# A bias tile of 512 bytes in place of 32, in an attention kernel with two expert layers

## The chip, the cores and the metric

The kernel runs on one core of a Trainium2 chip. The metric is the device time of one execution in microseconds (us), as the median of the runs shown. Engines are called as in the profile: PE is TensorE's matmul, PEld its weight load, DVE is VectorE, ACT is ScalarE, POOL is GpSimd, SP issues most of the DMAs. About 0.3% (3.1 us here) is what a measurement of this kernel can tell from no change.

## The reference

Attention with a compressive memory over 4 batches, 8 heads, 576 positions and 64 columns a head; its result, as 2304 tokens by 512 columns, goes through two expert layers.

```python
def _attn_ref(q, k, v, M_prev, z_prev, beta):
    scores = scale * q @ k.T                    # causal, softmax -> a
    local = a @ v
    q_p = phi(q)                                # elu + 1
    mem_out = (q_p @ M_prev) / (q_p @ z_prev + 1e-6)
    g = sigmoid(beta)
    return g * mem_out + (1 - g) * local

def _moe_ref(x, w_in, w_out):                   # 2304x512, 512x2048, 2048x512
    h = x @ w_in
    return (h * np.cos(h)) @ w_out

def _moe2_ref(x, w_in, w_out):                  # the same shapes
    h = x @ w_in
    r = np.maximum(h, 0.0)
    return (r * r) @ w_out
```

## The kernel before, in words

The first 206 us are attention: 16 units (a batch and a pair of heads), one after the other, each with its scores, exponentials, transposes and products. Its result goes to DRAM and comes back as the tiles of x. Beside attention run the first conversions of weights, which arrive as 64-bit floats.

Then come the expert layers. The tokens are cut into five blocks: 512, 512, 512, 256, 512 (blocks 0 to 4). The 2048 inner columns are cut into 16 groups f = 0 to 15. One step s is one block and one f: function l1 (matmuls at line 267, output h) makes 128 inner columns from x, functions g_a to g_g (lines 280 to 328) turn h into the expert function's value, split in a high part gh and a low part gl, and l2 (matmuls at line 762, output a) adds its product with w_out into accumulators. l2 runs two steps behind l1. The order of steps is block 0 with f 0 to 7, block 1 with all f, block 0 with f 8 to 15, then blocks 2, 3, 4; that is the first layer. The second layer takes blocks 0, 1, 2, 4, 3.

All matmuls of the expert layers work on pairs of high and low parts: high by high, high by low and low by high. For l1 a step has 4 x 3 = 12 matmuls. The stationary operand is a slice of 128 columns (512 bytes in a partition) of winh or winl of group f, the moving operand is xh or xl with 512 columns (256 in block 3). For l2 the first layer has 12 matmuls a step: stationary a slice of wouth or woutl, moving gh or gl. In the second layer the roles change: stationary is a slice of gh or gl, moving is wouth or woutl with 512 columns, and a step has 12 matmuls (6 in block 3, whose 256 tokens make two slices). PE runs the 12 of l1 of one step and the 12 of l2 of another in turns, at times with one dozen cut in two by the other.

Tiles lie in SBUF in the order in which their pools are made: wA (line 114: weights of f = 0 to 3), wr (115: raw and half-made weights), xs (116: x tiles, xh, xl), cst (117: halfpi alone, line 124), gp and g3 (276, 277: gf, ki, gh, gl), and then the pools of attention (336 to 338), which end with attention and make room for go (903: output tiles) and wB (904: weights of f = 4 to 15). Every tile of wA, wr, gp, g3, go and wB has a multiple of 512 bytes in a partition; the two of 2304 bytes in xs make 4608 together, and lie ahead of xh and xl. Only halfpi is smaller: 4 bytes, for which 32 are set aside.

```python
    cst = ctx.enter_context(tc.tile_pool(name="cst", bufs=1))
    NA = CFG["NA"]                          # 4
    wpool = [wA] * NF
    halfpi = cst.tile([128, 1], F32, name="halfpi")
...
    wB = ctx.enter_context(tc.tile_pool(name="wB", bufs=1))
    for f in range(NA, NF):
        wpool[f] = wB
```

So before the change wA, wr, xh and xl have one address mod 512, and gf, ki, gh, gl, the output tiles and the weights of f = 4 to 15 another, 32 bytes on.

The tile halfpi is written once by POOL (line 647) and read as the bias of the cosine (line 308).

Of the kernel before, what the change touches and what calls it, by code (L numbers as in the profile page):

```python
# [9 lines left out]
F32 = mybir.dt.float32  # L10
# [75 lines left out]
def kernel(  # L86
# [30 lines left out]
    cst = ctx.enter_context(tc.tile_pool(name="cst", bufs=1))  # L117
# [3 lines left out]
    NA = CFG["NA"]  # L121
    NSP = NF
    wpool = [wA] * NF
    halfpi = cst.tile([128, 1], F32, name="halfpi")
    wt = {}

    pe, act, dve, pool = nc.tensor, nc.scalar, nc.vector, nc.gpsimd
# [207 lines left out]
    def attention(ctx):  # L335
# [7 lines left out]
        pe, act, dve, pool = (_Pinned(tc, e) for e in (nc.tensor, nc.scalar, nc.vector, nc.gpsimd))  # L343
# [300 lines left out]
            )  # L644
        for t in (t[:, S:] for t in (*qpb, *Pl)):
            pool.memset(t, 0.0)
        pool.memset(halfpi, math.pi / 2)
        nc.scalar.dma_start(out=ig, in_=beta.rearrange("(o h) -> o h", o=1).partition_broadcast(128))

        def gates():  # L650
# [87 lines left out]
        pe, act, dve, pool = nc.tensor, nc.scalar, nc.vector, nc.gpsimd  # L738
# [162 lines left out]
    with ExitStack() as actx:  # L901
        attention(actx)
# [58 lines left out]
```

## Time and profile before

| | us |
|---|---|
| median of 3 runs | 1023.69 |
| lowest and highest run | 1021.48, 1024.98 |
| span of the profiled execution, first to last instruction | 1022.1 |
| PE busy in it | 997.3 |
| mean granted clock of PE | 0.995 |

The span is one execution; the runs are others. A busy share of PE counts a matmul up to a modelled end, so the time that a matmul takes of PE is read from the starts: a row of the chain of waits that holds 12 matmuls in a run lasts from the start of its first to the start of what comes next. The letters "PE h L267" stand for l1's matmuls and "PE a L762" for l2's. The granted clock is 1.00 at 2.4 GHz and 0.5 at 1.2 GHz.

### The profile page before, as it was taken

The numbers are of one execution on the slowest core, as the hardware profiler recorded it, in microseconds if no ns is written. First come the engines' busy times: TensorE is split into PE (matmuls) and PEld (weight loads), VectorE is DVE, ScalarE is ACT, GpSimd is POOL, SyncE is SP. The second block draws the span as 40 slices with busy tenths as digits, with TensorE's granted clock in tenths as the row PEclk, the third lists the DMA queues.
The fourth block names the chain that finished last, engine by engine and source line by source line (L and its number), as shares of the span: only waits on it lengthen the run. The fifth ranks groups of instructions, "written<-read, shape, count | busy, mean of one in ns | idle before, by whom it ended". The sixth has DMA issues, their size and how long they took to land.

```text
span 1022.1 us, 14853 instructions
## 1 busy us (share of the span) xinstructions
PE 997.3 (98%) x5456; PEld 800.8 (78%) x5456; DVE 597.1 (58%) x1217; ACT 545.3 (53%) x1120; POOL 240.1 (23%) x294
## 2 busy tenths in 40 slices
PE   8999999889999899999999999999999999999998
PEld 5777777667777688888997777888888888888897
DVE  6888898668998766446564799624222322322232
ACT  6988987677777565436565776413212322321232
POOL 5776865274331100000005544200000000000000
PEclk9999999999999999999999999999999999999999
DMA  6456655352435642002023235002000100100010
GB/s 203 142 155 187 208 195 162 116 184 83 144 119 191 201 139 73 1 1 83 1 63 113 83 102 196 21 1 62 21 1 20 53 1 1 52 1 1 1 42 21
DMA packets 53736, 88.00 MB, mean 86 GB/s; under 512 B 9504, under 2 KB 29344, under 8 KB 53664
## 3 DMA queue, kind: packets, MB, share of 16 engines
q1 hardware_dynamic: 53088, 86.57, 26.6%
q8 instruction: 43, 0.70, 0.3%
q10 hardware_dynamic: 576, 0.50, 0.1%
q14 instruction: 29, 0.24, 0.1%
HBM read 66.07 MB, written 20.97 MB: 85 GB/s over the span
## 4 chain that ended last, share of the span: by engine, by line
PE 74%; DVE 10%; ACT 6%; DMA 5%; issue 3%; POOL 2%; SPq 0%; DVEq 0%; ACTq 0%; POOLq 0%
PE h L267 29%; PE a L762 28%; PE o L47 5%; PE sps L47 5%; PE ptps L47 4%; PE qps L47 1%; DVE wb L169 1%; DVE gf L300 1%; DVE wa L173 1%; DMA xraw<-xT 1%; DMA wf<-ws2in 1%; DVE gl L325 1%; DVE wa L165 1%; DVE gf L292 1%; DMA wraw<-in_moe_w_in_dram 1%
## 5 line engine op out<-in xcount | busy, mean ns | idle before, releaser
L267 PE MATMUL h<-xh,winh 128*128 128x512 f32 (+1 forms) x628 | 234.5, 374 | 5.6 <-DVE gf L313 3.5
L267 PE MATMUL h<-xl,winh 128*128 128x512 f32 (+1 forms) x628 | 234.1, 373 | 0.0
L267 PE MATMUL h<-xh,winl 128*128 128x512 f32 (+1 forms) x628 | 233.7, 372 | 0.0
L325 DVE TENSOR_TENSOR gl<-gf,gh 128x512 fp32r<-128x512 f32 (+1 forms) x158 | 107.8, 683 | 124.1 <-ACT gh L318 123.9
L318 ACT ACTIVATE gh<-gf 128x512 fp32r<-128x512 f32 (+1 forms) x158 | 92.1, 584 | 113.4 <-PE a L762 95.8
L267 PEld LDWEIGHTS h<-xh,winh 128*128 128x128 f32 x628 | 118.2, 189 | 31.0 <-DVE gf L313 5.6
L267 PEld LDWEIGHTS h<-xh,winl 128*128 128x128 f32 x628 | 118.6, 189 | 22.6
L267 PEld LDWEIGHTS h<-xl,winh 128*128 128x128 f32 x628 | 118.5, 189 | 22.4
L296 DVE TENSOR_TENSOR gf<-gf 128x512 f32<-128x512 f32 (+1 forms) x80 | 53.5, 672 | 137.5 <-ACT gf L288 137.4
L288 ACT ACTIVATE gf<-h 128x512 f32<-128x512 f32 (+1 forms) x80 | 43.8, 552 | 153.0 <-PE h L267 152.4
L762 PE MATMUL a<-gl,wouth 128*128 128x512 f32 (+1 forms) x320 | 116.9, 372 | 3.0 <-DVE gl L325 3.0
L762 PE MATMUL a<-gh,woutl 128*128 128x512 f32 (+1 forms) x320 | 116.3, 369 | 0.0
L762 PE MATMUL a<-woutl,gh 128*128 128x512 f32 x288 | 112.9, 392 | 0.0
L762 PE MATMUL a<-wouth,gl 128*128 128x512 f32 x288 | 112.9, 392 | 0.0
L762 PE MATMUL a<-wouth,gh 128*128 128x512 f32 x288 | 98.7, 392 | 0.0
L762 PE MATMUL a<-gh,wouth 128*128 128x512 f32 (+1 forms) x320 | 86.3, 374 | 4.3 <-ACT gh L318 2.4
L47 POOL TENSOR_SCALAR P<-P,sm 128x512 f32<-128x512 f32 (+3 forms) x128 | 78.9, 634 | 38.4 <-DVE sm L47 22.2
L313 DVE TENSOR_TENSOR gf<-h,gf 128x512 f32<-128x512 f32 (+1 forms) x78 | 49.3, 633 | 52.5 <-PE h L267 37.9
L286 ACT ACTIVATE ki<-h 128x512 int32<-128x512 f32 (+1 forms) x77 | 42.1, 547 | 57.0 <-DVE gf L313 50.3
L762 PEld LDWEIGHTS a<-gl,wouth 128*128 128x128 f32 x320 | 60.2, 188 | 15.7 <-DVE gl L325 5.3
L762 PEld LDWEIGHTS a<-gh,wouth 128*128 128x128 f32 x320 | 56.4, 188 | 18.5 <-ACT gh L318 4.8
L47 ACT ACTIVATE P<-P,mx 128x384 f32<-128x384 f32 (+3 forms) x127 | 69.5, 551 | 0.0
(111 smaller groups left out, 1558.0 us busy)
## 6 DMA issues: line engine op xcount, KB each, us to landing
wraw<-in_moe_w_in_dram SPq DMA_DIRECT2D x32, 512.0 KB, 3.9
wraw<-in_moe_w_out_dram SPq DMA_DIRECT2D x32, 512.0 KB, 3.5
qk<-in_qk_dram SPq DMA_DIRECT2D x15, 640.0 KB, 5.4
vr<-in_vrow_dram SPq DMA_DIRECT2D x16, 320.0 KB, 4.4
xT<-x SPq DMA_DIRECT2D x16, 288.0 KB, 4.4
out_dram<-ob SPq DMA_DIRECT2D x17, 256.0 KB, 2.3
x1T<-ob SPq DMA_DIRECT2D x16, 256.0 KB, 2.9
xraw<-x1T SPq DMA_DIRECT2D x16, 256.0 KB, 2.7
```

The lines of the kernel that those rows point to most:

```text
L47: made = call(*args, **kwargs)
L165: lambda: dve.tensor_scalar(out=a, in0=a, scalar1=3, scalar2=0x3FFFFFF8, op0=ALU.logical_shift_left, op1=ALU.bitwise_and,),
L169: lambda: dve.scalar_tensor_tensor(out=b, in0=hi, scalar=-0x40000000, in1=a, op0=ALU.bitwise_and, op1=ALU.bitwise_or),
L173: lambda: dve.tensor_tensor(out=a, in0=b, in1=r, op=ALU.add),
L267: pe.matmul(out=h[:, 0:n], lhsT=lt[:, kk * 128:(kk + 1) * 128], rhs=rt[:, 0:n], start=(kk == 0 and x == 0), stop=(kk == KD - 1 and x == 2),)
L286: act.activation(out=kis[s], in_=hs[s], func=AF.Copy, scale=1.0 / TWO_PI)
L288: act.activation(out=rs[s], in_=hs[s], func=AF.Relu)
L296: dve.tensor_tensor(out=rs[s], in0=rs[s], in1=rs[s], op=ALU.mult)
L313: dve.tensor_tensor(out=rs[s], in0=hs[s], in1=rs[s], op=ALU.mult)
L318: act.activation(out=gh, in_=rs[s], func=AF.Copy)
L325: eng.tensor_tensor(out=gl, in0=rs[s], in1=gs[s].bitcast(F32), op=ALU.subtract)
L762: nc.tensor.matmul(out=o, lhsT=lt, rhs=rt, start=((p, j, f) in opens and x == 0), stop=((p, j, f) in closes and x == 2),)
```

## The change

The tile halfpi gets 128 columns in place of one, 512 bytes in place of 32, and the write of its value names its first column. All tiles that lie behind it start 480 bytes later.

```diff
@@ -121,7 +121,7 @@
     NA = CFG["NA"]
     NSP = NF
     wpool = [wA] * NF
-    halfpi = cst.tile([128, 1], F32, name="halfpi")
+    halfpi = cst.tile([128, 128], F32, name="halfpi")
     wt = {}
 
     pe, act, dve, pool = nc.tensor, nc.scalar, nc.vector, nc.gpsimd
@@ -644,7 +644,7 @@
             )
         for t in (t[:, S:] for t in (*qpb, *Pl)):
             pool.memset(t, 0.0)
-        pool.memset(halfpi, math.pi / 2)
+        pool.memset(halfpi[:, 0:1], math.pi / 2)
         nc.scalar.dma_start(out=ig, in_=beta.rearrange("(o h) -> o h", o=1).partition_broadcast(128))
```

## Rows read from the trace of the kernel before

**Rows 1.** Page, part 1: busy time, share of the span, instructions.
```profile
PE 997.3 (98%) x5456; PEld 800.8 (78%) x5456; DVE 597.1 (58%) x1217; ACT 545.3 (53%) x1120; POOL 240.1 (23%) x294
```

**Rows 2.** Busy time by stretches, PE alone: stretch, length, busy (matmuls), clock, DMA, GB/s.
```profile
206.00:356.00 150.00, 141.23 (x591) 0.99 0.47 151
342.90:346.40 3.50, 3.50 (x10) 0.51 0.13 20
346.40:494.00 147.60, 146.90 (x698) 1.00 0.21 70
...
556.00:621.00 65.00, 62.18 (x265) 1.00 0.34 105
621.00:1022.00 401.00, 397.21 (x1812) 1.00 0.08 28
```

**Rows 3.** Waits of PE, 206 to 356 us: total us, times, longest us.
```profile
PE h L267 <- DVE gf L313: 2.3, 2, 2.1
PE a L762 <- DVE gl L325: 2.1, 4, 1.1
```

**Rows 4.** Waits of PE, 540 us to the end.
```profile
PE h L267 <- DVE gf L313: 1.2, 1, 1.2
PE a L762 <- DVE gl L325: 1.0, 1, 1.0
```

**Rows 5.** Chain of waits, second layer: start us, us, what.
```profile
885.35 1.62 PE a L762 x7
886.97 2.75 PE h L267 x12
...
895.27 2.80 PE a L762 x12
898.07 2.73 PE h L267 x12
...
904.06 2.80 PE a L762 x12
909.20 2.80 PE h L267 x12
...
915.26 2.72 PE a L762 x12
...
926.34 2.72 PE a L762 x12
```

**Rows 6.** Chain of waits, first layer, block 2: two runs of 24.
```profile
422.87 5.60 PE h L267 x24
428.47 5.47 PE a L762 x24
```

**Rows 7.** Instructions on tile halfpi: count, then duration ns, minimum, median, maximum.
```profile
L47 POOL MEMSET halfpi<- x1: 92/92/92, 3.7 to 3.7; 128x1 f32 x1
```

**Rows 8.** Chain of waits, block 3 (256 columns) in both layers.
```profile
476.85 2.88 PE h L267 x24
...
496.33 2.84 PE h L267 x24
...
973.33 1.42 PE h L267 x12
```

**Rows 9.** Waits of DVE, 206 to 540 us.
```profile
DVE gf L313 <- PE h L267: 32.2, 17, 6.9
```

**Rows 10.** Groups of DVE, up to 206 us and from 206 to 610 us.
```profile
L47 DVE SCALAR_TENSOR_TENSOR wb<-wraw,wa 128x512 int32<-128x512 int32 x16 | 11.2, 698 | 0.0
...
L169 DVE SCALAR_TENSOR_TENSOR wb<-wraw,wa 128x512 int32<-128x512 int32 x38 | 29.6, 779 | 0.4
```

**Rows 11.** Attention: stretch, length, busy of PE, PEld, DVE, ACT, POOL, clock.
```profile
0.00:206.00 206.00, 198.01 (x1748) 144.89 (x1748) 167.53 (x548) 168.28 (x444) 123.45 (x192) 0.98 0.54 171
```

**Rows 12.** Timeline of PE after its longest wait: start us, us, instruction.
```profile
343.38 0.63 PE L267 MATMUL h<-xl,winh 128*128 128x512 f32 x1
343.81 0.63 PE L267 MATMUL h<-xh,winl 128*128 128x512 f32 x1
```

## The prediction, made before the changed kernel was run

> **What bounds the kernel now.** I read the page's busy times first: PE is busy 98% of the span [rows 1], far ahead of the others. A share says little of where PE is late, so next come the stretches. From 621 us on PE is busy to the end but for the tail of outputs (397.2 of 401 us), and from 346 to 494 us for 146.9 of 147.6; there every nanosecond of a matmul is a nanosecond of the kernel [rows 2]. From 206 to 356 us and from 556 to 621 us PE stands idle for 8.8 and 2.8 us, because DVE and ACT come late with gf, gl and gh [rows 2, 3, 4]; a faster PE may only wait longer there. Third, the chain of waits shows how long a dozen matmuls takes from start to start. That is the view that decides this case, because the kernel before already holds both kinds of addresses.
>
> Which kind a row is follows from the order of steps. In [rows 5], from the second layer's block 4, the h rows are f = 1, 3, 5 and the dozens of a are f = 0 and 1, 2, 4, 6 (the piece of 7 ahead of them is f = 15 of the block before). x and the weights of f < 4 have equal addresses mod 512, so h of f = 1, 3 is an equal pair and h of f = 5 an unequal one. For a it is the other way round: gh and gl lie 32 bytes on, equal to the weights of f >= 4, unequal to those of f < 4. The rows follow this both ways: h takes 2.75 and 2.73 us where equal and 2.80 where not, a takes 2.80 where unequal and 2.72 where equal [rows 5]. Of the 62 runs of exactly 12 between 621 and 966 us, 32 read 2.79 or 2.80 (the unequal ones) and 30 read 2.72 to 2.75 (the equal ones). The first layer, in which gh moves and the weight stands, shows the same: 24 of h with f = 7, 8 take 5.60 us, 24 of a with f = 5, 6 take 5.47 [rows 6]. The clock is 1.00 in all of them [rows 2].
>
> **The change, part by part.** The removed and added operations cost nothing: POOL's write stays one column, of 0.09 us at 3.7 us into the span, long before the first cosine [rows 7]. No instruction, wait or DMA is added or moved in the program's text. What changes is where tiles lie: gf, ki, gh, gl, the output tiles and the weights of f >= 4 move by 480 bytes, and then all operands of l1 and l2 are equal mod 512.
>
> *Matmuls that become equal pairs.* By the loops, a block of 512 tokens has 12 steps of 12 h (f >= 4) and 4 steps of 12 a (f < 4) that are unequal: 192 of 384. The first layer has four such blocks, 768; the second four and the 4 x 6 a of its block of 256, 792. An unequal one takes 2.80 / 12 = 233.3 ns. What an equal one will take is bounded by 2.75 and 2.72 us a dozen: 229.2 and 226.7 ns [rows 5]. Equal dozens that unequal ones cut in two are slower: a piece of 7 reads 1.62 us, 231.4 ns [rows 5]. After the change no unequal ones stand between, so I take a value near the faster end for all, 2.73 us, 227.5 ns. That is 5.8 ns for each: 4.45 us in the first layer, 4.6 us in the second.
>
> *Matmuls that are equal already.* The uninterrupted dozens average about 2.74 us, 228.3 ns, the pieces more, and by the same reasoning both come to 227.5: at least 0.8 ns each if so, 0 if not. The first layer has 768, the second 840 (768, and 72 in its block of 256): 0.6 and 0.7 us.
>
> *Matmuls with 256 moving columns.* Here the trace speaks against the change. 24 of h take 2.88 us with f = 1, 2 (equal) and 2.84 with f = 7, 8 (unequal) in the first layer; in the second, f = 1 (equal) takes 1.42 a dozen, as much as half of 2.84 [rows 8]. The first layer has 144 h and 48 a that become equal: 192 x 1.7 ns = 0.3 us lost. In the second I take nothing.
>
> *What the stages keep.* The second layer keeps all: after 621 us PE waits for nothing but the end [rows 2]; 4.6 + 0.7 = 5.3 us. In the first layer a block gains 192 x (5.8 + 0.8) ns = 1.27 us. Block 2 (378 to 470 us) lies in a stretch without idle time and keeps it [rows 2]. Blocks 0 and 1 (206 to 378 us) gain 2.5 us, but PE is there late by DVE's chain at several places, the longest 2.1 us at 342 us [rows 3]. DVE in turn waits for h for 32 us between 206 and 540 us [rows 9], so the stretch is paced by a ring of PE, ACT and DVE; nothing in the trace gives the share that is kept, the ends are 0 and all, and I take half, 1.25 us. For block 4 (520 to 608 us), with the conversion of the second layer's weights beside it and 2.8 us idle [rows 2, 4], again half, 0.65 us. Sum of the first layer: 1.27 + 1.25 + 0.65 = 3.2 us, between 1.27 and 5.1.
>
> *Tiles of attention.* All that PE reads in attention lies behind halfpi and moves together, so no pair of its operands changes. Conversions there read one tile that moves (wa) and one that doesn't (wraw): their distance mod 512 goes from 64 to 32 bytes. No row shows 32. The nearest are 698 ns at 64 and 779 at 0, the latter at other work on POOL [rows 10]: at most 0.08 us for each of three such operations in 16 units, 3.9 us of DVE's 167.5 busy us, beside PE with 198 of 206 busy [rows 11]. I take 0, since DVE has 38 us to spare; without that cover it would be up to 3.9 us either way.
>
> The sum: 5.3 + 3.2 - 0.3 = 8.2 us. The profiled span of 1022.1 becomes 1013.9; the median lies 1.6 us above that span, so the time is 1015.5 us.
>
> **A rule that speaks against it.** By the rows, a matmul takes 233.3 or 227.5 ns by where its operands lie. The Trainium skill's page "SBUF — State Buffer", section "Who interferes with whom", says that TensorE reads the moving operand and the weights through two independent ports and that PE never waits on anyone. By that rule addresses can't matter and the time stays 1023.7. The trace disagrees already: 2.80 against 2.72 to 2.75 us a dozen, 2 to 3%, with h and a in opposite parts of f. It is a rival below all the same.
>
> **The rivals.** *Unchanged, 1023.7 us.* The difference could go with something else that differs by f, such as where in SBUF a weight lies, or the matmuls could be slow for a neighbour's sake. For it speaks only the rule above. Against: on the same weights of f < 4, h is fast and a slow, and on f >= 4 the reverse, which no property of the weight tile alone makes. Chance 0.09.
>
> *The first layer gives all back and the equal pairs stay at 2.75, some 1020 us.* The second layer then earns 792 x 4.2 ns = 3.3 us, with the 0.3 of the narrow block 3.0, and block 2 of the first 0.8 more at best: 1019.9 to 1020.7. For it: the waits end by DVE and ACT [rows 3, 4]. Chance 0.22.
>
> *All is kept, and more, some 1012 us.* 5.3 + 5.1 - 0.3 = 10.1 us, and one dip of the clock less: at 343 us, after PE's longest wait, matmuls start 0.43 us apart in place of 0.23, at a granted clock of 0.5 (1.2 GHz), about 8 of them, 1.6 us [rows 2, 12]. Chance 0.12.
>
> *Slower, some 1028 us, by the clock.* A PE that is ahead waits longer for DVE. The trace has six waits of PE of 0.8 to 1.4 us after 206 us, three of them among those of [rows 3, 4], without such a dip, and one of 2.1 us with it. If the first layer's whole gain (5 us) turned into idle time at those places and each brought a dip of 1.6 us, 9.6 us would be lost against 5.0 gained in the second layer: 1028.3. It needs four dips to fall behind the time before, and six to be slower by over 0.3%. Chance 0.05.
>
> **How the numbers follow.** The forecast, a part of the first layer's gain kept (1013 to 1019 us), has 0.52. The range takes in its bounds and reaches to the rival of about 1020.7 above and of about 1012 below: 1011.8 to 1020.8. Faster by over 0.3% (under 1020.6): 0.52 + 0.22 + 0.12 = 0.86. Within 0.3%: 0.09. Slower: 0.05.
>
> **What would show it.** In the profile of the changed kernel, dozens of h and of a with 512 columns should read 2.72 to 2.75 us in the chain for every f, with no 2.80 left; the second layer, from the first h of its block 0 to the end, should be 5 us shorter; the busy time of PE should fall by about the sum and its waits between 206 and 356 us grow by a little over 1 us. Rows of 2.80 that stay for f >= 4 would prove the address rule wrong. Waits of PE that grow by as much as its matmuls shrink would prove the share kept wrong, and more stretches at a clock of 0.5 would bring the slow rival.

## The result and the profile after

The median of four runs is 1014.41 us (1011.35 to 1015.45), that of four runs of the kernel before, taken beside them, 1022.91 us (1021.48 to 1024.98): 8.5 us less. The ratio on record is 0.9904 with a 95% interval of 0.9882 to 0.9926; that of the two medians is 0.9917, inside it. The profiled execution of after has a span of 1013.2 us, 8.9 less than before. All engines run the same instructions in the same order as before; only the tiles behind halfpi have moved, by 480 bytes each.

The page of after, part 1 (busy us, share of the span, instructions), stands against [rows 1]:

```profile
PE 985.9 (97%) x5456; PEld 801.0 (79%) x5456; DVE 597.6 (59%) x1217; ACT 545.5 (54%) x1120; POOL 240.9 (24%) x294
```

PE's busy time fell by 11.4 us, more than the span: PE also stands idle 2.5 us longer. The other engines' times agree within 1 us. Where the new idle time lies is read from the stretches of after (length, busy time of PE with its matmuls, granted clock, DMA share, GB/s; of [rows 2] the last stretch is 9 us longer, as that kernel is):

```profile
206.00:356.00 150.00, 139.58 (x590) 0.99 0.49 157
...
346.40:494.00 147.60, 145.53 (x697) 0.99 0.20 68
...
556.00:621.00 65.00, 62.19 (x269) 1.00 0.33 108
621.00:1013.00 392.00, 388.28 (x1802) 1.00 0.08 27
```

From 206 to 356 us PE is idle for 10.4 us, where it was 8.8; from 621 us on it is idle for 3.7 us, tail and all, where it was 3.8. From 346.4 to 494 us it is idle for 2.1 us, where it was 0.7, but 0.8 of that is a wait for gh in block 3 that both kernels have, at 492.6 us here and at 494.6 before, and the rest lies ahead of block 2. So the second layer kept what it gained, and the first two blocks of the first layer did not keep all. Which waits grew shows the list of PE's waits of after from 206 to 356 us (total us, times, longest us; of before, in [rows 3] for the first two kinds):

```profile
PE a L762 <- ACT gh L318: 2.4, 4, 1.0
PE h L267 <- DVE gf L313: 2.4, 2, 1.4
PE a L762 <- DVE gl L325: 1.9, 3, 1.1
PE a L762 <- ACT ob L131: 1.8, 2, 1.4
PE h L267 <- DVE gf L292: 1.4, 1, 1.4
```

The waits for DVE's gf and gl are as they were (2.3 and 2.1 us in [rows 3]); those for ACT's gh and ob have grown, from 1.1 to 2.4 and from 1.2 to 1.8 us.

The view that decides is again the chain of waits. From the second layer's block 4 in after (start us, us, what), the rows that answer to [rows 5]:

```profile
868.59 2.72 PE h L267 x12
...
874.48 2.72 PE a L762 x12
...
887.63 2.72 PE a L762 x12
890.35 2.72 PE h L267 x12
...
901.23 2.72 PE h L267 x12
...
907.12 2.72 PE a L762 x12
```

Every whole dozen reads 2.72 us, h and a alike; of the 64 between 621 and 966 us one reads 2.75, and none 2.79 or 2.80. The same view of the first layer in after, blocks 2 and 3, answers to [rows 6] (2 x 24 of 512 columns, 5.60 and 5.47 us there) and [rows 8] (24 of h with 256 columns, 2.88 and 2.84 there):

```profile
421.44 5.44 PE h L267 x24
426.88 5.44 PE a L762 x24
...
474.67 2.87 PE h L267 x24
...
494.33 2.88 PE h L267 x24
```

The wide matmuls (512 columns) of these runs take 5.44 / 24 = 226.7 ns. Single dozens of the first layer still take more, such as that of a with f = 4 in block 2: 232 ns a matmul in after, and as much in e2 and e6 below. The narrow ones (256 columns) behind f >= 4 went up from 2.84 to 2.88 us for 24, as feared.

**Stage by stage.** The same matmul can be found in each trace by its place in the order of the program. The table holds the time from the first matmul of one stage to the first of the next (blocks 0 and 1, which are mixed, as one stage; it begins three steps into the layer, behind the noise of its start; the last column ends with the start of the last matmul), for the two kernels and for those of the experiments below that are otherwise whole. "Dips" counts stretches of a granted clock of 0.5 inside blocks 0 and 1 of the profiled run.

| kernel | blocks 0, 1 | dips there | block 2 | block 3 | block 4 | layer 2, 512 | layer 2, 256 |
|---|---|---|---|---|---|---|---|
| before | 168.79 | 1 | 88.42 | 50.65 | 87.89 | 357.90 | 51.61 |
| after | 168.47 | 1 | 87.01 | 51.07 | 87.11 | 351.44 | 51.69 |
| after, again | 168.51 | 1 | 87.01 | 51.06 | 87.57 | 351.47 | 51.69 |
| e2_all_32 | 167.03 | 0 | 87.00 | 51.06 | 87.79 | 351.67 | 51.69 |
| e6_halfpi_256 | 166.52 | 0 | 86.94 | 51.06 | 87.73 | 351.59 | 51.69 |
| e9_narrow_8 | 169.21 | 1 | 87.02 | 51.09 | 87.18 | 351.51 | 51.68 |
| e3_wB_off | 167.25 | 0 | 88.83 | 50.75 | 88.12 | 358.92 | 51.95 |
| e4_g_off | 169.96 | 1 | 88.45 | 50.88 | 88.02 | 357.74 | 51.99 |

After minus before, left to right: -0.3, -1.4, +0.4, -0.8, -6.5, +0.1, together -8.5 us; another 0.4 us or so lies ahead of these stages.

### The profile page after: what moved, and what is told of

Same layout as the page of the kernel before. It is cut to its first block, busy times and chain, and to the rows that moved or that the text cites. A ratio compares the mean times of both kernels' runs of the same rounds, so it can differ in the third digit from the quotient of the medians.

```text
span 1013.2 us, 14853 instructions
## 1 busy us (share of the span) xinstructions
PE 985.9 (97%) x5456; PEld 801.0 (79%) x5456; DVE 597.6 (59%) x1217; ACT 545.5 (54%) x1120; POOL 240.9 (24%) x294
## 3 DMA queue, kind: packets, MB, share of 16 engines
q1 hardware_dynamic: 53088, 86.57, 26.3%
## 4 chain that ended last, share of the span: by engine, by line
PE 74%; DVE 10%; ACT 6%; DMA 5%; issue 3%; POOL 2%; SPq 0%; DVEq 0%; ACTq 0%; POOLq 0%
PE a L762 29%; PE h L267 28%; PE o L47 5%; PE sps L47 5%; PE ptps L47 4%; PE qps L47 1%; DVE gf L300 1%; DVE wb L169 1%; DMA wf<-ws2out 1%; DMA ws2in<-wa 1%; DVE gl L325 1%; DVE wa L173 1%; ACT wa L149 1%; DVE gf L292 1%; DVE wa L165 1%
## 5 line engine op out<-in xcount | busy, mean ns | idle before, releaser
L267 PE MATMUL h<-xh,winh 128*128 128x512 f32 (+1 forms) x628 | 231.5, 369 | 5.5 <-DVE gf L313 4.1
L267 PE MATMUL h<-xl,winh 128*128 128x512 f32 (+1 forms) x628 | 231.0, 368 | 0.0
L267 PE MATMUL h<-xh,winl 128*128 128x512 f32 (+1 forms) x628 | 230.8, 367 | 0.0
```

The lines of the kernel that those rows point to most:

```text
L267: pe.matmul(out=h[:, 0:n], lhsT=lt[:, kk * 128:(kk + 1) * 128], rhs=rt[:, 0:n], start=(kk == 0 and x == 0), stop=(kk == KD - 1 and x == 2),)
```

## The experiments

**e1_curve: is it the distance, and with which period?** Matmuls alone, 32 in a group, with two moving and four stationary slices in turn, each slice a multiple of 512 bytes from the last; d bytes are added to the place of every weight.

```diff
+    for n, name in ((512, "wide"), (256, "half")):
+        for d in [32 * x for x in range(33)] + [4, 8, 16, 24, 48]:
+            ...
+            for i in range(32):
+                mm(o, n, 512 * (i % 2), 1024 + d // 4 + 128 * (i % 4))
```

> Only a measurement of matmuls; attention and both expert layers are left out, so its time is no kernel's. PE alone runs groups of 32 matmuls, each with its own weight load, for 512 and then 256 moving columns. In a group the address of the weights is d bytes past that of the moving operand mod 512, d = 0 to 1024 in steps of 32 and 4, 8, 16, 24, 48. Theory (equal addresses mod 512 alone are the fast case): at 512 columns 227 ns from start to start at d = 0, 512 and 1024, 233 at every other d. Rival 1 (a shorter period, say 64 or 128): also 227 at its multiples. Rival 2 (the traces' difference comes from work on other engines beside PE): one value at every d. Two groups more: in 'own' a moving operand is equal to its own weights and 32 bytes off the next ones', in 'next' the reverse; if a matmul is slowed by the weight load that runs beside it (the next one's), 'next' is at 227 and 'own' at 233. At 256 columns, 120 ns at d = 0 and 118 elsewhere.

The chain of waits of e1_curve (a group's name ends with its d in letters, a for 0 to j for 9: aadc is 32, abjc 192, acfg 256, afbc 512, aaai 8):

```profile
19.41 7.26 PE wideaaaa L60 x32
26.67 7.46 PE wideaadc L60 x32
...
63.98 7.33 PE wideabjc L60 x32
...
78.77 7.26 PE wideacfg L60 x32
...
138.13 7.26 PE wideafbc L60 x32
...
320.80 3.84 PE halfaaaa L60 x32
...
445.16 3.71 PE halfaaai L60 x32
```

So the difference is there without any other engine at work: 226.7 ns from start to start at d = 0, 256, 512, 768 and 1024, 232 to 234 at the other multiples of 32 but 192, which has 228.9. The period is 256 bytes, half of what the change's description and my prediction had, and the curve between is no step: 232.5 at 4 bytes, 231 at 8, 230 at 24. With 256 columns equal operands are not the best: 120 ns against 116 at 8 bytes and 117 to 118 at most others (120 at 128 and 160). In the two groups in which the load ahead alternates, neither order gives 227 ns (231.7 and 231.5), so that "the load that runs beside a matmul alone counts" falls.

**e2_all_32: equality or place?** The change, with a tile of 32 bytes ahead of wA, so that all operands are 32 bytes further on and still equal.

```diff
-    wA = ctx.enter_context(tc.tile_pool(name="wA", bufs=1))
+    lead = ctx.enter_context(tc.tile_pool(name="lead", bufs=1)); nc.gpsimd.memset(lead.tile([128, 8], F32, name="lead")[:, 0:1], 0.0); wA = ctx.enter_context(tc.tile_pool(name="wA", bufs=1))
```

> The changed kernel with 32 bytes set aside ahead of all tiles, so every address is 32 bytes on and all operands of l1 and l2 are still equal. Theory (equality counts, not the place): every dozen of 512 columns at 2.72 us, span 1013 us as in the changed kernel. Rival (a tile's own place mod 512 or mod 64 counts): dozens at 2.75 to 2.80 us, span up to 1022 us.

A single run took 1013.33 us. By f, the wide matmuls of both layers average 226.7 to 227.5 ns (226.7 to 227.6 in after), and the stages behind blocks 0 and 1 are within 0.7 us of those of after (table). So moving all by 32 bytes doesn't count; equality does.

**e3_wB_off: equality taken away again.** The change, with 32 bytes ahead of wB, so that the weights of f >= 4 lie 32 bytes off everything else.

```diff
-    wB = ctx.enter_context(tc.tile_pool(name="wB", bufs=1))
+    pad = ctx.enter_context(tc.tile_pool(name="pad", bufs=1)); nc.gpsimd.memset(pad.tile([128, 8], F32, name="pad")[:, 0:1], 0.0); wB = ctx.enter_context(tc.tile_pool(name="wB", bufs=1))
```

> The changed kernel with 32 bytes set aside between the output tiles and the weights of f >= 4: x, gh, gl and the weights of f < 4 are equal, the weights of f >= 4 alone lie 32 bytes off. Theory: h and a of f < 4 stay at 2.72 us a dozen, h and a of f >= 4 both go to 2.80; by the loops 1152 h and 1224 a become unequal, 2376 x 6.4 ns = 15.2 us of PE, so 1024 to 1029.6 us by how much the first layer hides. Rival (the tile of gf, gh and gl or work on other engines set the pace of a): a stays at 2.72 for f >= 4, and the time at 1021.

1023.95 us, ratio to before 1.0014 (0.9997 to 1.0032): the whole gain is gone, with halfpi still at 512 bytes. In the chain of e3_wB_off the second layer's dozens of a and h with f < 4 are fast and those with f >= 4 slow:

```profile
885.27 2.76 PE h L267 x12
...
893.59 2.74 PE a L762 x12
896.34 2.72 PE h L267 x12
...
907.33 2.80 PE h L267 x12
...
913.36 2.80 PE a L762 x12
```

The second layer's wide blocks take 358.92 us, 1.0 more than before; of the 384 matmuls of a block 288 are unequal now, where before 192 were. The time came out just under what was expected, and the first layer has a part in that: its blocks 0 and 1 took 167.25 us, within 0.7 of e2 and e6, in which all are equal and no dip falls there either, though a matmul there takes 232.3 ns against 227.2.

**e4_g_off: do 480 bytes do it elsewhere?** The kernel before, with the 480 bytes put behind gp and g3 and ahead of wB. Then all of h is equal and all of a is not.

```diff
-    wB = ctx.enter_context(tc.tile_pool(name="wB", bufs=1))
+    pad = ctx.enter_context(tc.tile_pool(name="pad", bufs=1)); nc.gpsimd.memset(pad.tile([128, 120], F32, name="pad")[:, 0:1], 0.0); wB = ctx.enter_context(tc.tile_pool(name="wB", bufs=1))
```

> The kernel before (halfpi of 32 bytes) with 480 bytes set aside between the output tiles and the weights of f >= 4: x and all weights are equal, gh and gl alone lie 32 bytes off. Theory: every dozen of h at 2.72 us, every dozen of a at 2.80; 1632 a are unequal, 1632 x 6.4 ns = 10.4 us above the changed kernel at most, so 1021 to 1025 us, though 480 bytes were added as in the change. Rival (the 480 bytes ahead of the weights of f >= 4 make the gain): 1014 us.

1023.25 us, ratio 1.0001 (0.9986 to 1.0016). In its chain h and a differ for every f:

```profile
872.83 2.79 PE a L762 x12
...
877.94 2.75 PE h L267 x12
...
883.93 2.79 PE a L762 x12
...
889.04 2.75 PE h L267 x12
```

Two things follow. The place of gh against the weights is what pays. And equal dozens between unequal ones read 2.75 us (229.2 ns a matmul), not the 2.72 of after: unequal neighbours cost the equal ones something.

**e5_curve2: a finer curve, and mixed neighbours.** As e1, in steps of 8 bytes, and six patterns of 48 in which equal and unequal operands alternate.

```diff
+        for d in [8 * x for x in range(33)]:
...
+        ("ownequal", lambda i: 8 * (i % 2), lambda i: 8 * (i % 2)),
...
+        ("fourfour", lambda i: 0, lambda i: 8 * (i // 4 % 2)),
```

> Only a measurement of matmuls, as the first curve; all work of the reference is left out. Distances from 0 to 256 bytes in steps of 8, 32 matmuls each, at 512 and at 256 moving columns. The first curve repeated every 256 bytes, not every 512. Theory (period 256, both of its neighbouring weight loads count for a matmul): at 512 columns 226.7 ns at 0 and 256, 229 at 192, else 230 to 234; at 256 columns 116 at 8 and 117 to 122 elsewhere. Then six groups of 48. 'movealt' (the moving operand alternates between equal and 32 bytes off, weights fixed) and 'loadalt' (weights alternate): if both neighbours count, all matmuls are slow, 231 to 234, in each; if the next weight load alone counts, one in two is at 227. 'ownequal' and 'nextequal' (one of the two neighbours equal, the other 32 off): 231 to 234 both. 'fourfour' (four weights equal, four not): 227 within the equal four, 233 within the others. 'loadsame' (the same weights every time, 32 off): 233; rival, a load of the same weights costs nothing: 227 or less.

With 512 columns 120 bytes are as good as 0 and 256, and 240 nearly so; in the chain of e5_curve2 (abca is 120, acea 240, abci 128):

```profile
131.41 7.27 PE wideabca L60 x32
138.68 7.44 PE wideabci L60 x32
...
242.61 7.30 PE wideacea L60 x32
```

In the patterns no equal matmul is at 227: four equal and four unequal in turns repeat 236, 231, 229, 235, 232, 236, 224, 231 ns; pairs that are equal, each with the next one shifted by 32 bytes in both operands, take 233.3. The same weights every time, 32 bytes off, read 233.2, so that a repeated load isn't free of it. So "only a matmul's own and its next load's distance count" isn't borne out. With 256 columns 64 bytes gave 113.3 ns here and 117.8 in e1: there the pace depends on more than d.

**e6_halfpi_256: half the padding.** 256 bytes for halfpi instead of 512.

```diff
-    halfpi = cst.tile([128, 128], F32, name="halfpi")
+    halfpi = cst.tile([128, 64], F32, name="halfpi")
```

> The changed kernel with halfpi at 256 bytes, half of the change's. The operands of l1 and l2 are then equal mod 256, but 256 bytes apart mod 512. Theory after the curve (period 256): as the changed kernel, dozens at 2.72 us for every f, 1013 to 1016 us, and faster than the kernel before by 0.8 to 1.2%. Rival (the change's own words, equality mod 512): dozens of 2.80 where f is unequal, 1022 us.

1014.61 us, ratio 0.9907 (0.9876 to 0.9939), and 226.7 to 227.6 ns by f for the wide matmuls: the same as the change. "Equal mod 512" is more than it takes; equal mod 256 suffices.

**e7_light_before and e8_light_after: does DVE pace the first layer?** Both kernels without three of DVE's operations in each weight conversion that runs beside the expert layers.

```diff
-            for op in ops[2:3]:
+            for op in ():
...
-            for op in (ops[3], ops[5]) if ops else ():
+            for op in ():
```

> The kernel before without the three DVE operations of each weight conversion that runs beside the expert layers (lines 165, 169 and 173 there; the weights so made are not the reference's). About 2.0 us of DVE less for each of some 48 conversions. Theory (the first layer is paced by DVE, so it hides most of what faster matmuls earn): PE's waits between 206 and 356 us fall from 8.8 us to under 4, and the time by 5 us or more, to 1012 to 1018. Rival (the waits come from ACT's order or from DMAs): waits of 8 us stay, 1021 us or more.

> The changed kernel without the same three DVE operations (weights are not the reference's). Theory: with DVE out of the way the first layer keeps what the matmuls earn there, 1536 matmuls: 768 x 6.5 ns and 768 x 1.9 ns, less 0.3 us of the narrow block, 6.1 us, beside 6.6 in the second: 11.5 to 13 us less than the kernel before without them. Rival (the first layer is paced by something else): 8 to 9.5 us less, as in the change itself.

Both became slower: 1032.67 us, ratio 1.0085 (1.0055 to 1.0116), and 1025.34, ratio 1.0018 (0.9998 to 1.0038). DVE's busy time from 206 to 356 us fell from 126 to 74 us, and PE waited more, for ACT. In the waits of e7_light_before, of PE from 206 to 640 us and of ACT from 206 to 356 us:

```profile
PE a L762 <- ACT gh L318: 13.7, 5, 5.3
...
ACT wc L172 <- DMA wraw<-in_moe_w_in_dram: 15.6, 13, 2.5
ACT wc L172 <- DMA wraw<-in_moe_w_out_dram: 10.6, 10, 2.4
```

With DVE's share gone the conversion runs into its DMAs; ACT, in whose order wc stands, waits for raw weights while gh stands behind it, and PE waits for gh. Each has three dips of the clock behind 206 us (two of 3.4 us and one of 6.8 in e7, one of 3.4 and two of 6.8 in e8). The expectations fell: e8 less e7 is -7.3 us, no more than the change gave, and blocks 0 and 1 are no shorter (173.75 and 174.79 us, the latter with 3.4 us more at the low clock), while the second layer's wide blocks are (356.28 and 349.45). What paces these blocks with DVE's work in place the two don't show, as the conversions wait for their DMAs instead. The edit also shows that a lighter engine may cost time, by what it lets an ordered queue wait for.

**e9_narrow_8: a version for both widths?** The change, with block 3's moving operands in columns 62 to 317 of their tiles, so that the weight lies 8 bytes on from them mod 256, where e1 has 116 ns.

```diff
-                    rhs=rt[:, 0:n],
+                    rhs=rt[:, 62:62 + n] if n < 512 else rt[:, 0:n],
...
+        gh = g_3.tile(...)[:, (c := 62 if n < 512 and steps[s][0] == 1 else 0):c + n]
```

> The changed kernel, with the operands of 256 columns moved inside their tiles of 512: xh and xl of block 3, and gh and gl of block 3 in the first layer, stand in columns 62 to 317, which puts the weights 8 bytes past them mod 256. Theory from the curves (256 columns: 119.7 to 120 ns at equal addresses, 115.6 at 8): 384 h and 192 a in block 3 take 115.6 ns, 576 x 4.3 = 2.5 us less than the changed kernel, 24 in a row 2.78 us in place of 2.88, and the time 1011 to 1013. Rival (the curve's 8 bytes hold only where nothing else precedes): 2.88 stays and the time with it, 1014.

1012.51 us (1010.11 to 1013.72), ratio 0.989 (0.9867 to 0.9914), which the interval doesn't tell from the change, and no gain is in the trace: block 3 takes 51.09 us as against 51.06, and the chain of e9_narrow_8 has the old 2.88:

```profile
498.74 2.88 PE h L267 x24
501.62 2.88 PE a L762 x24
```

The expectation of 2.78 fell, though the time lies in its range: by luck, as two of these five runs had a granted clock of 1.0 and none of the six of the change beside them (e10) had more than 0.998. e12 says why no gain came.

**e10_after_again.** The change, nothing else, beside e9.

> The changed kernel once more, beside e9 on the same chip. All theories: 0.988 to 0.993 of the kernel before, 1013 to 1016 us. It is the mark for e9: a gain of 2.5 us there is 0.25%.

1015.18 us (1013.45 to 1016.52), ratio 0.9921 (0.9902 to 0.994). The stages agree with those of after to 0.1 us but for block 4 (0.5): it is the table's measure of its own error.

**e11_cut_blocks_0_1: what does PE's work weigh there?** The change without the product of xh with the low part of the weights in l1 of blocks 0 and 1: 32 steps x 4 matmuls x 226.9 ns = 29.0 us of PE less.

```diff
-            for x, (lt, rt) in enumerate(((hi, xh), (hi, xl), (lo, xh))):
+            for x, (lt, rt) in enumerate(((hi, xh), (hi, xl), (lo, xh))[:2 if p == 1 and j < 2 else 3]):
...
```

> The changed kernel without l1's third product (winl by xh) in the first layer's blocks 0 and 1; its h there is a little off the reference's. 32 steps x 4 matmuls x 227 ns take 29 us from PE between 206 and 378 us. Theory (that stretch is paced by the conversions beside it, their loads, stores and DVE and ACT operations, not by PE): it gets shorter by under 9 us, and PE's waits there grow by 20 us or more; from 378 us on all as in the changed kernel; 1005 to 1014 us. Rival (PE paces it, with chance waits between): 20 to 29 us shorter, 985 to 995 us.

A single run took 992.88 us. Blocks 0 and 1, as in the table, fell from 168.5 to 148.6 us. Of the 128 matmuls left out 12 lie ahead of this stage, and the other 116 make 26.3 us. Of these 19.9 are kept, or 18.0 to 18.5 against e2 and e6, which have no dip there, as e11 has none. PE's idle time in the stage (what passes from one start to the next beyond 245 ns, the slow matmuls of a dip with it) grew from 14.7 us in after, and 12.9 and 13.4 in e6 and e2, to 20.6. The waits of PE in e11_cut_blocks_0_1 from 206 to 640 us show what takes the rest, the same three as ever; 5.4, 4.4 and 1.8 us of them lie before 356 us:

```profile
PE h L267 <- DVE gf L313: 7.0, 9, 1.2
PE a L762 <- ACT gh L318: 6.5, 6, 1.8
PE a L762 <- DVE gl L325: 3.0, 6, 1.1
```

So the conversions don't set the pace of this stretch by themselves: some 70% of what PE has less to do is kept, and its waits take the rest.

**e12_dozens: neighbours and place, by themselves.** Matmuls alone again: dozens of equal and unequal ones (32 bytes) in turns, then 48 each with the moving operand, the weight, or both moved by 8 or 248 bytes (load: the weight 8 bytes up; move and moveup: the moving operand 248 and 8 bytes up; both and bothfar: both 8 and 248 bytes up).

```diff
+        for name, s in (("equal", 0), ("unequal", 8)):
...
+            ("none", 0, 0), ("load", 0, 2), ("move", 62, 0), ("moveup", 2, 0), ("loadup", 0, 62),
+            ("both", 2, 2), ("bothfar", 62, 62), ("last", 0, 0),
```

> The kernel is replaced by matmuls on one tile, so its output and its whole time mean nothing; only the pitch (start to start) is read. First part: dozens of 512-column matmuls, equal operands (distance 0) and unequal ones (32 bytes) in turns, eight of each. Theory (the pace remembers several matmuls): as in the dozens of the kernel before, the first five or so of an equal dozen behind an unequal one still take about 230.5 ns and only the later ones 226.9, so an equal dozen reads 2.74 to 2.75 us and an unequal one 2.80. Rival (only the next load counts): all of an equal dozen but its last take 226.7, 2.72 to 2.73 us. Second part: 48 matmuls each where the moving operand is moved (by 248 or by 8 bytes), or the weight, or both, in 512 and 256 columns. Theory (the distance alone sets the pace): moving operand 248 bytes up reads as weight 8 bytes up (231 ns at 512 columns, 115.6 at 256), and both moved by the same amount reads 226.7 and 120.0. Rival (the place of the moving operand itself counts too, for which speaks that block 3 stayed at 120 ns with its moving operand 248 bytes up): 256 columns with the moving operand up by 248 bytes read 119 to 120 ns, and with the weight up by 8 bytes 115.6.

The chain of e12_dozens:

```profile
23.12 2.79 PE unequala L60 x12
25.92 2.73 PE equalb L60 x12
...
64.60 10.89 PE widenone L60 x48
75.49 11.07 PE wideload L60 x48
86.56 11.35 PE widemove L60 x48
...
120.23 11.07 PE wideboth L60 x48
131.30 11.21 PE widebothfar L60 x48
...
153.40 5.75 PE halfnone L60 x48
159.15 5.55 PE halfload L60 x48
164.70 5.76 PE halfmove L60 x48
170.46 5.63 PE halfmoveup L60 x48
```

In the dozens only the edges pay: the first matmul of an equal dozen takes 231 ns, the last, ahead of an unequal one, 235, the ten between 226.7, and the dozen 2.73 us. That is the rival's number; the theory of a longer memory falls for these operands. The second part goes the other way. The weight 8 bytes up and the moving operand 248 bytes up have the same distance and read 230.7 and 236.7 ns; both 8 or both 248 bytes up have the distance 0 and read 230.4 and 233.3. So the distance alone doesn't set the pace: the place counts too, though not when all is moved by 32 bytes (e2). With 256 columns the weight 8 bytes up gives 115.5 ns and the moving operand 248 bytes up gives 120.0, which is what block 3 did in e9: that move doesn't help, though it makes the same distance. Moved up by 8 bytes instead, the moving operand gives 117.3; no run tried that in the kernel.

## Why the prediction was right, point by point

The forecast of 1015.5 us lies 1.1 us above the measured 1014.41, and the sum of 8.2 us beside 8.5. Its terms did not all come out so well: the second layer gained 1.1 us more than forecast and blocks 0 and 1 about 1 us less, so that the sum is as close as it is in part by luck.

*Which matmuls are slow, and that they cease to be.* Right: in the second layer no 2.80 is left for any f. e2, e3 and e4 make the cause the addresses and not the place of the weights or the amount of padding: 32 bytes ahead of wB bring the old time back with the padded halfpi still there. The rule of the Trainium skill's page "SBUF — State Buffer", section "Who interferes with whom" (independent ports, PE waits on no one), read as the prediction read it, that addresses can't matter, does not hold here: 233.3 against 226.7 ns while nothing but PE works (e1, e12). The measurement decides. What the description of the change and I both had wrong is the period, 256 bytes and not 512 (e1, e6); it made no difference to the time, since 512 is a multiple.

*The second layer, 5.3 us.* Of the forecast, 5.1 us were for the wide blocks, and these gained 6.5. Both terms of it were sized too small; the mean pitches (start to start, waits left out) in those blocks, before and after, show by how much. The unequal ones went from 233.5 ns (576 of h) and 233.1 (192 of a) to 226.7 and 226.8: 5.1 us, where 768 x 5.8 ns were 4.5. I had put 227.5 for an equal matmul with no unequal ones near. The larger miss is the matmuls that were equal already: they went from 229.8 ns (192 of h) and 228.7 (576 of a) to the same 226.7 and 226.8, 1.7 us, where I gave 0.8 ns each, 0.6 us. (The two make 6.8, a little above the 6.5 that the stage shows.) By its place in a run of like matmuls, an equal h of the kernel before takes 230.7, 233.0, 228.9, 230.9 and 231.9 ns in the first five places, 226.4 to 230.0 in the next six, and 234.0 in the twelfth; in after each of the twelve has 226.4 to 227.0. The number for this stood in [rows 5], the piece of 7 with 231.4 ns. I named the unequal ones beside it as the cause, and then priced the gain by the uncut dozens, which most of PE's work there is not. Why five places pay here and one at each edge in e12 stays open; in the kernel both operands of the neighbouring dozen are other tiles, in e12 only the weight moves. Unequal addresses are not needed for it: in after, where all are equal, each of the 19 runs of wide matmuls right behind narrow ones starts with about 233, 236, 228, 233 and 231 ns before it reads 227, and in e5 the equal group at 256 bytes, right behind the one at 248, starts with 235, 229, 232, 231 and 228.

*The first layer, 3.2 us less 0.3.* Block 2 gained 1.4 us beside 1.27, and block 4 0.8 and, in the second profile, 0.3, beside 0.65. The narrow block lost 0.4 beside 0.3; the second layer's, for which I took nothing, lost 0.1. The step that failed is the half that blocks 0 and 1 keep: 1.25 us were forecast, and 0.3 is what the two profiles of after show against the one of before, each with one dip of the clock. All-equal kernels without a dip there take 167.03 and 166.52 us (e2, e6), those with one 168.47 to 169.21 (after, e9, e10): a dip goes with about 2 us, several times the gain of this stage. The matmuls themselves did get faster there, from 231.0 to 227.2 ns, 2.4 us in all. The ring of PE, ACT and DVE took 2.0 of it back as idle time: PE's in this stage (as in e11) grew from 12.7 to 14.7 us, the share of ACT in it by gh and ob. I had named DVE's chain as what makes PE late; the waits that grew are ACT's, and with work taken off DVE the stretch gets no shorter (e7, e8). What does take so small a gain nearly whole, when some 18 of 26.3 us are kept in e11, the runs don't settle.

*The rivals.* "Unchanged" is out by e3 and e4. "All given back in the first layer" was half right: blocks 0 and 1 gave back nearly all, but block 2, where PE is hardly idle, nothing. "All kept, and a dip less": in the profiled run the dip didn't go, it moved from 343 to 353 us (270 us in e10), and it is missing in those of e2 and e6. But single runs of one kernel differ in this too, and the mean granted clock sorts their times: at 0.999 and 1.0 the kernel before takes 1018.6 to 1022.1 us (12 of its runs beside the experiments) and the all-equal ones (after, e2, e6, e10) 1011.3 (2 runs); at 0.994 they take 1024.0 to 1026.1 (10 runs) and 1014.9 to 1015.5 (2 runs). So the gain is 9 to 10 us at either end and not the dips' doing. The slower rival needed four dips more; none came.

*What would have shown it.* The second layer's dozens read as announced, and the second layer is 6.4 us shorter, where 5 were announced. Two markers were off. PE's busy time fell by 11.4 us and not by about the sum, as what a stage doesn't keep leaves the busy time too, for idle time; and the waits between 206 and 356 us grew by 1.6 us, but at ACT's gh and ob, not at DVE's gf and gl.

## What to carry to other kernels

Where PE sets the end, read the time of a dozen matmuls from start to start in the chain of waits and sort it by tile: a pattern by tile that no wait explains may be one of addresses, and here 256 bytes in one small tile were worth 0.8%. A gain of nanoseconds on each matmul is whole where PE never waits (the second layer, block 2) and may vanish where it waits now and then; so price it by stage, with the idle time of each. Mind a second shape that likes it the other way: 256 columns lost 1 to 2 ns by what 512 columns gained 6 by.

## What was not expected of the hardware

- For 128x512 fp32r operands the pitch of matmuls is 226.7 ns where moving and stationary operand have equal addresses mod 256 bytes and 230 to 234 at most other distances; 120 bytes give 226.7 as well, 240 bytes 228 and 192 bytes 229 (e1, e5).
- Equal distance isn't the whole of it: both operands 8 bytes up give 230.4 ns, both 248 up 233.3 (e12); with all tiles 32 up the kernel keeps 226.7 to 227.5 (e2).
- With 256 columns equal operands take 120.0 ns and a weight 8 bytes up 115.5; the moving operand moved alone by 248 bytes, the same distance, changes nothing (120.0), by 8 bytes it gives 117.3 (e12).
- Unequal neighbours cost equal matmuls up to five places in the kernel before (229 to 233 ns), and one at each edge in e12 (231 and 235 ns). Narrow matmuls ahead of wide ones cost the first five places too with all operands equal (228 to 236 ns, after).
- A dip of the clock to 0.5 comes and goes between runs of one kernel and of kernels that differ in a few bytes; blocks 0 and 1 are about 2 us longer with one than without. The runs of before span 1018.6 us (mean granted clock 1.0) to 1026.1 (0.994).
